# Linear attention into a gated attention layer: three products on quarters of the array's columns, feature weights first, other order

## Chip, cores and metric

The kernel runs on one core of a Trainium2 chip. The metric is the time of one execution in microseconds, measured on the device; lower is better. The engines of the core work side by side: TensorE (matmuls, PE in the rows; PEld are its weight loads), VectorE (DVE), ScalarE (ACT), GpSimd (POOL) and SyncE (SP), which issues the transfers here.

## What is computed

Eight batches of eight heads with 576 positions go through a linear attention, and its result through a layer of four masked attention experts, of which a gate takes two for each position. All is in f32.

```python
def phi(x):                                   # 64 -> 2 * 128 features
    proj = np.einsum('bhsd,df->bhsf', x, w_phi)
    proj = proj - np.max(np.abs(proj), axis=-1, keepdims=True)
    return np.concatenate([np.exp(proj), np.exp(-proj)], axis=-1)
q_p, k_p = (phi(q), phi(k))
kv = np.einsum('bhsf,bhsd->bhfd', k_p, v)
z = np.sum(k_p, axis=2)
num = np.einsum('bhsf,bhfd->bhsd', q_p, kv)
den = np.einsum('bhsf,bhf->bhs', q_p, z)[..., None] + 1e-06
x = num / den                                 # then (8, 576, 512)
...
logits = x @ w_gate                           # weights w of the best 2 of 4
for e in range(E):
    q, k, v = x @ wq[e], x @ wk[e], x @ wv[e]
    scores = np.where(causal, -1e9, scale * (q @ k.transpose(0, 2, 1)))
    a = softmax(scores)
    ye = a @ v @ wo[e]
    ...                                       # out += w * ye where e was taken
```

## The kernel before

The heads are taken in 32 pairs (`NPAIRS`, four to a batch); a pair has one head in partitions 0 to 63 and one in 64 to 127. For each pair `stream_k` projects the keys with the feature weights `wf` (L435 on two halves of the array's rows, the last 64 positions at L251), centres them on DVE and takes both exponentials on ACT into `ek`. `stream_kv` then multiplies the features with the values (L506), adds the sums over the keys (L523, the `z` of the reference, partly summed beforehand on DVE into `zs`), copies the result to `kvt`, transposes it (L532) and copies it to `kv`. `stream_q` projects the queries (L435), GpSimd finds the largest value over the features (L569), and DVE and ACT make the features `mx` and `u`. `stream_n` multiplies these with `kv`: first the denominators (L598), which go through a small transfer, a reciprocal and a broadcast on GpSimd, then the numerators (L607), which `divide` turns into `xh` and `xl`.

After four pairs a batch is complete. `stream_b` projects it for the experts (L251), makes the scores (L739, L251) and the exponentials `a`; `stream_t` scales and transposes these (L889), and `attend` multiplies them with the values `vs` (L920), 16 times in all. `project_out` (L251) ends the batch.

A matmul whose output has 64 partitions uses half of the array's columns, one with 32 a quarter; products that lie on different parts of the columns run side by side. Before, L506, L607 and L920 are on halves, L523 and L598 on quarters, L435 and L739 on two halves of the rows, and all else on the full array. I call each of these a tiling, and the step from one to another a change of tiling. One f32 product appears as two records of a weight load and a matmul. The sizes over positions are `PARTS`, 256 and 320.

The order of the work on each engine is fixed while the program is built. A `Plan` holds its own estimate of every engine's clock; each stream offers its next step with a position (`rank(p)` plus an entry of `POS1` or `NPOS`, or `at_batch(b)` plus one of `POS`, in units of a pair), and `loop` takes the ready step with the lowest position. A step on another tiling than the last one is put back by `OTHER`. While the first pairs fill the pipeline, `keep_warm` puts small matmuls without use into the gaps of TensorE; the last of them stands before the first finished pair. SP issues all loads in one queue, `load_phi` (the feature weights `wf`) among them, at position -5.

Of the kernel before, what the change touches and what calls it, by code (L numbers as in the profile page):

```python
# [39 lines left out]
ZEROS = 1.27   # L40

POS1 = {'k': -0.42, 'q': 0.49, 'v': 0.57, 'kv': 0.99, 'z': -1.95, 'cen': 0.77, 'evu': 0.02, 'ph0': -0.35, 'ph1': 0.01, 'div': 2.37, 'evd': -0.81, 'lk': -1.73, 'lq': -1.32} 
BOFF = (0.86, -0.14, 1.03, 0.96, 0.98, 0.78, -0.42, -2.05)

ORDER = (('p0', 'v0', 's0', 'p1', 's1'), ('p0', 'v0', 's0', 'p1', 's1'))
POS = {'p0': 7.38, 'p1': -0.11, 'v0': 7.93, 'gate': 6.05, 's0': 3.18, 's1': 6.21, 't0': 5.46, 't1': 9.4, 'out': 14.46} 
# [180 lines left out]
def tile_linear_attn_moe(ctx, tc, qt, kt, v, wts, out):  # L227
# [265 lines left out]
    def stream_kv():  # L493


        for p in range(NPAIRS):
# [3 lines left out]
            kc, ps = yield Step('PE', ekk + [vk], 'c', lambda: ('phi_k', p) in done and ('load_v', p) in done, tiling=(128, 64)), rank(p) + POS1['kv']  # L500
# [77 lines left out]
    def stream_n():  # L578


        for p in range(NPAIRS):
# [19 lines left out]
            for s0, s1 in PARTS:  # L601
                pk, ps = yield Step('PE', Pk + [kvk], 'c', has('rb', p), tiling=(128, 64)), rank(p) + NPOS[1]
                n = s1 - s0
                for c in range(2):
                    for h in range(2):
                        plan.run('PE', 2 * n / TRATE + 3, [pk], Pk + [kvk], tiling=(128, 64))
# [298 lines left out]
    def attend(b, g, pos):  # L905
# [7 lines left out]
        for s0, s1 in PARTS:  # L913
            pk, ps = yield Step('PE', AT, 'c', ready, tiling=(128, 64)), pos + SLOPE[3]
            js = range(0, (s1 + 127) // 128)
            for j in js:
                q0 = max(s0, 128 * j)
                for e in range(2):
                    plan.run('PE', 2 * (s1 - q0) / TRATE + 3, [pk], [f'vs{j}'] + AT, tiling=(128, 64))
# [113 lines left out]
```

## Time and profile before

| | |
|---|---|
| three runs | 659.52, 659.72, 660.65 us; median 659.72 |
| the profiled execution's own time | 662.2 us |
| span in that execution, first to last instruction | 660.4 us |
| TensorE, DVE, ACT, GpSimd busy | 98%, 81%, 72%, 31% of the span |
| mean granted TensorE clock | 1.000 |

The profile shows one execution. Times within it are counted from the span's start. A row of the timeline merges neighbouring records of one line, gives their count after the x, and the start of the first; the starts of two blocks that follow each other on TensorE give the duration of the first one with its change of tiling.

### The profile page before, as it was taken

To read this page: it belongs to the slowest core of one execution; us is meant where nothing else is said; L and a number is where in the kernel's file an instruction comes from. 1 tells how busy PE (TensorE), PEld (TensorE's weight loads), DVE (VectorE), ACT (ScalarE), POOL (GpSimd) and SP (SyncE) were. 2 spreads that over 40 slices of the span, in tenths; PEclk is the share of its full clock that TensorE was granted. 3 is DMA by queue.
4 is the path that set the end of the run, shared out by engine and by line. 5 is a ranking of instruction groups with operands and counts; after the bars stand their busy time and mean duration, and the time that the engine had idled before them with its cause. 6 is when DMAs were issued, how large, how long until landed. Compare 5 with 4: busy or idle time off the path is not lost.

```text
span 660.4 us, 16266 instructions
## 1 busy us (share of the span) xinstructions
PE 644.9 (98%) x6050; PEld 507.9 (77%) x6050; DVE 538.1 (81%) x1459; ACT 474.7 (72%) x1212; POOL 207.6 (31%) x154
## 2 busy tenths in 40 slices
PE   8999999999999999999999999999999999999997
PEld 7665677677887787777778787877888788888886
DVE  6889998889999778979899886997878986865562
ACT  4765868969777758668769885685877787765574
POOL 4717743172116162115332432122330523010000
PEclk9999999999999999999999999999999999999999
DMA  5643321021104022122221321113211210010011
GB/s 168 179 142 112 98 61 40 23 77 51 51 21 150 22 79 59 59 77 77 61 60 58 103 70 53 50 33 120 61 40 42 57 55 4 2 51 25 1 73 73
DMA packets 38752, 43.53 MB, mean 66 GB/s; under 512 B 19088, under 2 KB 21648, under 8 KB 38672
## 3 DMA queue, kind: packets, MB, share of 16 engines
q1 hardware_dynamic: 38672, 42.49, 21.8%
q8 instruction: 48, 0.79, 0.5%
q14 instruction: 32, 0.26, 0.1%
HBM read 32.58 MB, written 9.44 MB: 64 GB/s over the span
## 4 chain that ended last, share of the span: by engine, by line
PE 62%; DVE 19%; ACT 11%; issue 3%; DMA 2%; POOL 1%; SPq 1%; DVEq 0%; ACTq 0%
PE ps_c L251 21%; PE ps_c L607 7%; PE ps_c L506 7%; PE ps_c L435 7%; PE ps_c L889 6%; PE ps_c L920 5%; PE ps_c L598 4%; ACT a L262 3%; PE ps_c L739 3%; DVE ps_c L760 2%; DVE zs L465 2%; ACT ek L262 2%; DVE u L571 2%; DVE pmax L479 2%; PE ps_c L523 2%
## 5 line engine op out<-in xcount | busy, mean ns | idle before, releaser
L569 POOL PARTITION_ALL_REDUCE mx<-u x64 | 140.7, 2257 | 186.9 <-ACT u L260 180.7
L251 PE MATMUL ps_c<-xh,qk 128*128 128x320 f32 (+1 forms) x512 | 104.0, 294 | 0.0
L262 ACT ACTIVATE a<-ps_c,nm 128x256 f32<-128x256 f32 (+4 forms) x160 | 81.6, 526 | 27.0 <-DVE nm L760 15.0
L251 PEld LDWEIGHTS ps_c<-xh,qk 128*128 128x128 f32 x512 | 82.4, 188 | 0.4 <-DVE pmax L479 0.4
L262 ACT ACTIVATE ek<-ek 128x1152 f32<-128x1152 f32 x64 | 75.2, 1174 | 5.9 <-DVE ek L482 5.5
L639 POOL PARTITION_BROADCAST xf<-dr x32 | 30.7, 958 | 150.4 <-DMA dr<-dc 115.7
L506 PE MATMUL ps_c<-ek,v_in 128*64 128x256 f32 x640 | 75.1, 381 | 0.1
L251 PE MATMUL ps_c<-xl,qk 128*128 128x256 f32 (+1 forms) x256 | 75.1, 293 | 0.0
L760 DVE CUSTOM_DVE_ANT_0 ps_c<-ps_c,mask 128x128 f32<-128x128 f32 (+2 forms) x144 | 66.5, 517 | 2.1 <-PE ps_c L739 1.8
L479 DVE TENSOR_REDUCE pmax<-ps_c 128x4 f32<-128x512 f32 (+1 forms) x96 | 50.3, 547 | 20.0 <-PE ps_c L435 19.8
L506 PEld LDWEIGHTS ps_c<-ek,v_in 128*64 128x64 f32 x640 | 45.0, 137 | 27.0 <-ACT ek L262 1.1
L571 DVE TENSOR_TENSOR u<-u,mx 128x576 f32<-128x576 f32 x64 | 61.5, 970 | 4.1 <-POOL mx L569 4.0
L251 PE MATMUL ps_c<-vg,xh 128*128 128x260 f32 (+1 forms) x320 | 59.2, 286 | 0.0
L260 ACT COPY u<-ps_c 128x320 f32<-128x320 f32 (+1 forms) x122 | 40.9, 422 | 23.4 <-PE ps_c L435 23.1
L251 PE MATMUL ps_c<-yh,wo 128*128 128x256 f32 (+1 forms) x256 | 52.1, 298 | 1.4 <-ACT a L262 1.4
L889 PE MATMUL ps_c<-ident,a 128*128 128x128 f32 x400 | 49.7, 276 | 2.9 <-ACT a L262 2.2
L262 ACT ACTIVATE mx<-u 128x576 f32<-128x576 f32 x64 | 44.6, 696 | 10.2 <-DVE u L571 10.2
L889 PEld LDWEIGHTS ps_c<-ident,a 128*128 128x128 f32 x400 | 43.9, 141 | 9.6 <-ACT a L262 5.3
L482 DVE TENSOR_TENSOR ek<-ps_c,pmax 128x512 f32<-128x512 f32 (+1 forms) x96 | 50.9, 548 | 0.4
L260 ACT COPY at<-ps_c 128x128 f32<-128x128 f32 (+3 forms) x150 | 48.5, 460 | 0.7 <-PE ps_c L889 0.4
L251 PEld LDWEIGHTS ps_c<-xl,qk 128*128 128x128 f32 x256 | 48.1, 188 | 0.0
L251 PEld LDWEIGHTS ps_c<-vg,xh 128*128 128x128 f32 (+1 forms) x320 | 47.7, 178 | 0.1
(137 smaller groups left out, 1534.8 us busy)
## 6 DMA issues: line engine op xcount, KB each, us to landing
v_in<-in_v_dram SPq DMA_DIRECT2D x32, 320.0 KB, 3.0
q_in<-in_qt_dram SPq DMA_DIRECT2D x64, 144.0 KB, 2.9
out_dram<-ot SPq DMA_DIRECT2D x32, 288.0 KB, 2.2
k_in<-in_kt_dram SPq DMA_DIRECT2D x32, 160.0 KB, 2.9
k_in<-in_kt_dram SPq DMA_DIRECT2D x32, 128.0 KB, 2.8
dc<-dr SPq DMA_DIRECT2D x128, 2.2 KB, 1.9
ot<-in_wts_dram SPq DMA_DIRECT2D x5, 288.0 KB, 2.9
k_in<-in_kt_dram SPq DMA_DIRECT2D x32, 32.0 KB, 2.3
```

Of the source, the lines that this page charges most:

```text
L251: nc.tensor.matmul(o, a, b, start=start, stop=stop, skip_group_check=True)
L260: nc.scalar.copy(o, i)
L262: nc.scalar.activation(o, i, func, **kw)
L435: nc.tensor.matmul(o, a, b, start=True, stop=True, skip_group_check=True)
L479: dve(n * 128, [mk], [pk]).tensor_reduce(out=m[:, us], in_=src, axis=AX.X, op=ALU.max, apply_absolute_value=True)
L482: dve(n * 128, [f'ek{p % EKB}1'], [pk, mk]).tensor_tensor(out=ek2[p % EKB][:, 1, us, :], in0=src, in1=m[:, us].unsqueeze(2).to_broadcast([ ...
L506: nc.tensor.matmul(o[64 * h:64 * h + 64], v_in[:, 4 * h + t if t < 4 else 8 + h, :], ek[:, :, u_, :], start=t == 0, stop=t == 4, skip_grou ...
L569: nc.gpsimd.partition_all_reduce(M, U, 128, bass_isa.ReduceOp.absmax)
L571: dve(S, [uk], [mk], port=True).tensor_tensor(out=U, in0=U, in1=M, op=ALU.subtract)
L607: nc.tensor.matmul(ps[64 * h:64 * h + 64, 0:n], kvi[:, c, 64 * h:64 * h + 64], P_[h][c][:, s0:s1], start=c == 0, stop=c == 1, skip_group_c ...
L760: dve(n, [('nm', g, c), pk], [pk]).tensor_tensor_reduce(out=src, in0=src, in1=m, scale=-1.0, scalar=3.0e38, op0=ALU.add, op1=ALU.min, accu ...
L889: nc.tensor.transpose(ps[:, n * 128:(n + 1) * 128], a_blk[c][:, j, :], ident)
```

## The change

The three products on halves are each divided into two on quarters, over the same operands, and the plan's costs follow. The feature weights' load moves to position -50, ahead of all others. The numbers that set the order (`HOT`, `SLOPE`, `NPOS`, `FLEX`, `POS1`, `BOFF`, `POS`, `HEAD`, `OTHER`) are others; of these the diff keeps a few lines.

```diff
-HOT = 4.41 
-SLOPE = (0.61, 1.58, 5.89, 0.14, 0.85) 
+HOT = 4.2 
+SLOPE = (1.17, 1.58, 5.87, 0.13, 0.98) 
...
-HEAD = 4.01
+HEAD = 2.83
-OTHER = 2.37
+OTHER = 3.21
...
             for t in range(NJ):
                 for h in range(2):
                     u_ = 4 * h + t if t < 4 else 8
-                    plan.run('PE', 2 * 256 / TRATE + 3, [kc], ekk + [vk], tiling=(128, 64))
-                    nc.tensor.matmul(o[64 * h:64 * h + 64], v_in[:, 4 * h + t if t < 4 else 8 + h, :], ek[:, :, u_, :],
-                                     start=t == 0, stop=t == 4, skip_group_check=True)
+                    for k in range(2):
+                        g = slice(64 * h + 32 * k, 64 * h + 32 * k + 32)
+                        plan.run('PE', 256 / TRATE + 2, [kc], ekk + [vk], tiling=(128, 32))
+                        nc.tensor.matmul(o[g], v_in[:, 4 * h + t if t < 4 else 8 + h, 32 * k:32 * k + 32], ek[:, :, u_, :],
+                                         start=t == 0, stop=t == 4, skip_group_check=True)
...
                 for c in range(2):
                     for h in range(2):
-                        nc.tensor.matmul(ps[64 * h:64 * h + 64, 0:n], kvi[:, c, 64 * h:64 * h + 64],
-                                         P_[h][c][:, s0:s1], start=c == 0, stop=c == 1, skip_group_check=True)
+                        for g in range(64 * h, 64 * h + 64, 32):
+                            nc.tensor.matmul(ps[g:g + 32, 0:n], kvi[:, c, g:g + 32], P_[h][c][:, s0:s1], start=c == 0, stop=c == 1,
+                                             skip_group_check=True)
...
                 for e in range(2):
-                    nc.tensor.matmul(ps[64 * e:64 * e + 64, q0 - s0:s1 - s0], vs[j][:, g, e, :], ats[j][:, e, q0 - 128 * j:s1 - 128 * j],
-                                     start=j == 0, stop=j == js[-1], skip_group_check=True)
+                    for k in range(2):
+                        nc.tensor.matmul(ps[64 * e + 32 * k:64 * e + 32 * k + 32, q0 - s0:s1 - s0], vs[j][:, g, e, 32 * k:32 * k + 32],
+                                         ats[j][:, e, q0 - 128 * j:s1 - 128 * j], start=j == 0, stop=j == js[-1], skip_group_check=True)
...
-    for gen, pos in ((load_phi(), -5), ...
+    for gen, pos in ((load_phi(), -50), ...
```

In the changed kernel the lines shift: L506, L523, L532, L598, L607, L739, L889 and L920 become L508, L525, L534, L600, L610, L742, L892 and L924.

The first place is SP's queue at the start of the program, before; a row is one issue of a transfer, to the left of the arrow where it goes (`k_in`, `q_in` and `v_in` are keys, queries and values of a pair).

```order
L283 DMA k_in_105<-in_kt_dram 64x640
L283 DMA k_in_105<-in_kt_dram 64x512
L283 DMA k_in_105<-in_kt_dram 64x128
L283 DMA q_in_107<-in_qt_dram 64x576 x2
L283 DMA wf<-in_wts_dram 128x128
L283 DMA k_in_106<-in_kt_dram 64x640
L283 DMA k_in_106<-in_kt_dram 64x512
L283 DMA k_in_106<-in_kt_dram 64x128
L283 DMA q_in_108<-in_qt_dram 64x576 x2
L283 DMA v_in_109<-in_v_dram 128x640
```

The feature weights stand sixth, behind the first pair's keys and queries. The same queue in the changed kernel:

```order
L283 DMA wf<-in_wts_dram 128x128
L283 DMA k_in_105<-in_kt_dram 64x640
L283 DMA k_in_105<-in_kt_dram 64x512
L283 DMA k_in_105<-in_kt_dram 64x128
L283 DMA q_in_107<-in_qt_dram 64x576 x2
L283 DMA k_in_106<-in_kt_dram 64x640
L283 DMA k_in_106<-in_kt_dram 64x512
L283 DMA k_in_106<-in_kt_dram 64x128
L283 DMA v_in_109<-in_v_dram 128x640
L283 DMA q_in_108<-in_qt_dram 64x576 x2
```

They now stand first, and the second pair's queries come behind the first pair's values.

The second place is TensorE's queue around the 21st pair's product of features and values, before (`ps_c` are the banks of PSUM; the size is output partitions by columns, and x4 counts matmuls in a row).

```order
L739 MATMUL ps_c_66<-kkh_176,ql_173 128x384
L506 MATMUL ps_c_65<-ek_111,v_in_109 64x256 x10
L523 MATMUL ps_c_65<-zs,ones 32x128 x4
L607 MATMUL ps_c_67<-mx_138,kv_122 64x256
...
L607 MATMUL ps_c_68<-u_131,kv_122 64x320
L598 MATMUL ps_c_62<-mx_140,kv_123 32x256
...
L598 MATMUL ps_c_64<-u_133,kv_123 32x320
L739 MATMUL ps_c_61<-kkh_176,qh_172 128x512
```

The tilings follow as row halves, column halves, quarters, column halves, quarters, row halves; the transposes of this `kvt` (L532) come 90 rows behind L523. The same pair in the changed kernel:

```order
L742 MATMUL ps_c_63<-kkh_176,ql_173 128x512
L610 MATMUL ps_c_61<-mx_138,kv_122 32x256 x2
...
L610 MATMUL ps_c_66<-u_131,kv_122 32x320 x2
L600 MATMUL ps_c_68<-mx_140,kv_123 32x256
...
L600 MATMUL ps_c_62<-u_133,kv_123 32x320
L508 MATMUL ps_c_65<-ek_111,v_in_109 32x256 x20
L525 MATMUL ps_c_65<-zs,ones 32x128 x4
L435 MATMUL ps_c_61<-wf,k_in_106 128x128
...
L251 MATMUL ps_c_66<-wf,k_in_106 128x128
L534 MATMUL ps_c_65<-ident,kvt 128x128 x3
```

Numerators, denominators, features by values and key sums now follow each other on quarters, and the transposes of `kvt` come 13 projections behind the key sums.

## Rows read from the trace of the kernel before

**Rows 1.** The page's busy time of each engine (us, share of the span, instructions), and its chain of work that ended last, as shares of the span by engine and by line.

```profile
PE 644.9 (98%) x6050; PEld 507.9 (77%) x6050; DVE 538.1 (81%) x1459; ACT 474.7 (72%) x1212; POOL 207.6 (31%) x154
...
PE 62%; DVE 19%; ACT 11%; issue 3%; DMA 2%; POOL 1%; SPq 1%; DVEq 0%; ACTq 0%
PE ps_c L251 21%; PE ps_c L607 7%; PE ps_c L506 7%; PE ps_c L435 7%; PE ps_c L889 6%; PE ps_c L920 5%; PE ps_c L598 4%; ACT a L262 3%; PE ps_c L739 3%; DVE ps_c L760 2%; DVE zs L465 2%; ACT ek L262 2%; DVE u L571 2%; DVE pmax L479 2%; PE ps_c L523 2%
```

**Rows 2.** Windows: the stretch in us and its length, then busy time (and instructions) of PE, PEld, DVE, ACT and POOL, the granted clock, the share of the DMA engines, GB/s.

```profile
60.00:120.00 60.00, 58.57 (x525) 42.73 (x525) 56.08 (x136) 46.77 (x107) 31.47 (x22) 1.00 0.22 60
...
240.00:360.00 120.00, 118.80 (x1101) 94.41 (x1099) 106.29 (x284) 89.35 (x225) 43.06 (x31) 1.00 0.23 68
360.00:480.00 120.00, 119.72 (x1135) 93.80 (x1133) 101.08 (x269) 89.76 (x228) 36.38 (x26) 1.00 0.23 67
```

**Rows 3.** Groups of instructions by line, operation and shape: their count, busy time in us and mean ns of one, and the idle time before them.

```profile
L506 PE MATMUL ps_c<-ek,v_in 128*64 128x256 f32 x640 | 75.1, 381 | 0.1
...
L262 ACT ACTIVATE ek<-ek 128x1152 f32<-128x1152 f32 x64 | 75.2, 1174 | 5.9 <-DVE ek L482 5.5
```

**Rows 4.** TensorE's timeline from 284.9 to 293.2 us: start, duration to the last end, line, operands, rows*columns of the array, operand size, count of records. L607 stands between two blocks on halves.

```profile
284.92 2.93 PE L920 MATMUL ps_c<-at,vs 128*64 128x256 f32 x28
287.67 0.60 PE L607 MATMUL ps_c<-mx,kv 128*64 128x256 f32 x4
...
289.62 2.33 PE L506 MATMUL ps_c<-ek,v_in 128*64 128x256 f32 x20
291.87 0.42 PE L523 MATMUL ps_c<-zs,ones 128*32 128x128 f32 x8
292.12 0.38 PE L598 MATMUL ps_c<-mx,kv 128*32 128x256 f32 x1
...
292.33 0.38 PE L598 MATMUL ps_c<-mx,kv 128*32 128x256 f32 x1
...
292.55 0.43 PE L598 MATMUL ps_c<-mx,kv 128*32 128x320 f32 x1
...
293.20 1.16 PE L435 MATMUL ps_c<-wf,k_in 64*128 64x128 f32 x16
```

**Rows 5.** The same view from 246.9 us: L607 comes from the full array and goes on to L506.

```profile
246.90 0.65 PE L607 MATMUL ps_c<-mx,kv 128*64 128x256 f32 x4
...
248.89 0.82 PE L506 MATMUL ps_c<-ek,v_in 128*64 128x256 f32 x6
```

**Rows 6.** The same view from 337.2 us: L506, L523, L607 and L598, each with another tiling than the one ahead of it.

```profile
337.23 2.38 PE L506 MATMUL ps_c<-ek,v_in 128*64 128x256 f32 x20
339.54 0.43 PE L523 MATMUL ps_c<-zs,ones 128*32 128x128 f32 x8
339.89 0.65 PE L607 MATMUL ps_c<-mx,kv 128*64 128x256 f32 x4
...
341.98 0.40 PE L598 MATMUL ps_c<-mx,kv 128*32 128x256 f32 x1
...
342.22 0.38 PE L598 MATMUL ps_c<-mx,kv 128*32 128x256 f32 x1
...
342.44 0.43 PE L598 MATMUL ps_c<-mx,kv 128*32 128x320 f32 x1
...
343.09 0.50 PE L739 MATMUL ps_c<-kkh,qh 64*128 64x512 f32 x2
```

**Rows 7.** The timeline of all engines from the start of the span; SPq rows are issues of transfers, in brackets the idle time before and what ended it.

```profile
0.72 1.86 SPq L283 DMA_DIRECT2D k_in<-in_kt_dram  x3
...
2.62 1.24 SPq L283 DMA_DIRECT2D q_in<-in_qt_dram  x2
...
3.90 0.59 SPq L283 DMA_DIRECT2D wf<-in_wts_dram  x1
...
6.40 2.08 PE L435 MATMUL ps_c<-wf,k_in 64*128 64x128 f32 x16 [1.02 <-DMA wf<-in_wts_dram]
...
8.24 2.04 PE L435 MATMUL ps_c<-q_in,wf 64*128 64x256 f32 x8
...
10.83 15.89 POOL L569 PARTITION_ALL_REDUCE mx<-u  x7 [8.83 <-ACT u L260]
```

**Rows 8.** The page's DMA issues: transfer, count, KB each, median us from issue to landing.

```profile
q_in<-in_qt_dram SPq DMA_DIRECT2D x64, 144.0 KB, 2.9
...
k_in<-in_kt_dram SPq DMA_DIRECT2D x32, 160.0 KB, 2.9
k_in<-in_kt_dram SPq DMA_DIRECT2D x32, 128.0 KB, 2.8
```

**Rows 9.** TensorE's waits: who waited for whom, us in total, times, the longest in us.

```profile
PE ps_c L251 <- ACT a L262: 3.1, 4, 1.4
PE ps_c L532 <- ACT kvt L260: 2.4, 3, 1.1
PE ps_c L889 <- ACT a L262: 2.2, 6, 0.7
```

**Rows 10.** ACT's timeline: one copy of the products of features and values out of PSUM.

```profile
328.26 0.48 ACT L260 COPY kvt<-ps_c 128x384 f32<-128x384 f32 x1
```

**Rows 11.** The chain that ended last, in order of time (start, us, what): the projections of a pair's keys and queries.

```profile
293.27 2.06 PE ps_c L435 x24
```

More of the change, by code (lines that the diff above doesn't have):

```diff
@@ L28 @@
 PXB = 6
-HOT = 4.41
-SLOPE = (0.61, 1.58, 5.89, 0.14, 0.85)
-NPOS = (-0.32, 2.07)
+HOT = 4.2
+SLOPE = (1.17, 1.58, 5.87, 0.13, 0.98)
+NPOS = (1.07, 2.1)
 UB = 4
 AB = 1
-FLEX = (154, -44)
+FLEX = (151, -50)
 QB = 1
@@ L40 @@
 ZEROS = 1.27
-POS1 = {'k': -0.42, 'q': 0.49, 'v': 0.57, 'kv': 0.99, 'z': -1.95, 'cen': 0.77, 'evu': 0.02, 'ph0': -0.35, 'ph1': 0.01, 'div': 2.37, 'evd': -0.81, 'lk': -1.73, 'lq': -1.32}
-BOFF = (0.86, -0.14, 1.03, 0.96, 0.98, 0.78, -0.42, -2.05)
+POS1 = {'k': -0.42, 'q': 0.3, 'v': 0.35, 'kv': 0.68, 'z': -1.84, 'cen': 1.1, 'evu': 0.51, 'ph0': -0.21, 'ph1': 0.01, 'div': 2.66, 'evd': -0.83, 'lk': -1.07, 'lq': -0.41}
+BOFF = (0.78, 1.0, 1.0, 1.02, 0.8, 0.67, -0.27, -2.25)
 ORDER = (('p0', 'v0', 's0', 'p1', 's1'), ('p0', 'v0', 's0', 'p1', 's1'))
-POS = {'p0': 7.38, 'p1': -0.11, 'v0': 7.93, 'gate': 6.05, 's0': 3.18, 's1': 6.21, 't0': 5.46, 't1': 9.4, 'out': 14.46}
+POS = {'p0': 7.06, 'p1': 1.33, 'v0': 9.25, 'gate': 5.43, 's0': 3.27, 's1': 6.09, 't0': 3.9, 't1': 9.4, 'out': 14.92}
 NPAIRS = B * NP
-HEAD = 4.01
+HEAD = 2.83
 ADDS = (0, 2)
@@ L499, in stream_kv @@
             ek, ekk = ek2[i], [f'ek{i}0', f'ek{i}1']
-            kc, ps = yield Step('PE', ekk + [vk], 'c', lambda: ('phi_k', p) in done and ('load_v', p) in done, tiling=(128, 64)), rank(p) + POS1['kv']
+            kc, ps = yield Step('PE', ekk + [vk], 'c', lambda: ('phi_k', p) in done and ('load_v', p) in done, tiling=(128, 32)), rank(p) + POS1['kv']
             o = ps[:, 0:256].rearrange("p (c f) -> p c f", c=2)
@@ L601, in stream_n @@
             for s0, s1 in PARTS:
-                pk, ps = yield Step('PE', Pk + [kvk], 'c', has('rb', p), tiling=(128, 64)), rank(p) + NPOS[1]
+                pk, ps = yield Step('PE', Pk + [kvk], 'c', has('rb', p), tiling=(128, 32)), rank(p) + NPOS[1]
                 n = s1 - s0
@@ L605, in stream_n @@
                     for h in range(2):
-                        plan.run('PE', 2 * n / TRATE + 3, [pk], Pk + [kvk], tiling=(128, 64))
-                        nc.tensor.matmul(ps[64 * h:64 * h + 64, 0:n], kvi[:, c, 64 * h:64 * h + 64],
-                                         P_[h][c][:, s0:s1], start=c == 0, stop=c == 1, skip_group_check=True)
+                        for g in range(64 * h, 64 * h + 64, 32):
+                            plan.run('PE', n / TRATE + 2, [pk], Pk + [kvk], tiling=(128, 32))
+                            nc.tensor.matmul(ps[g:g + 32, 0:n], kvi[:, c, g:g + 32], P_[h][c][:, s0:s1], start=c == 0, stop=c == 1,
+                                             skip_group_check=True)
                 plan.spawn(divide(p, s0, s1, pk, ps), rank(p) + POS1['div'])
@@ L913, in attend @@
         for s0, s1 in PARTS:
-            pk, ps = yield Step('PE', AT, 'c', ready, tiling=(128, 64)), pos + SLOPE[3]
+            pk, ps = yield Step('PE', AT, 'c', ready, tiling=(128, 32)), pos + SLOPE[3]
             js = range(0, (s1 + 127) // 128)
@@ L918, in attend @@
                 for e in range(2):
-                    plan.run('PE', 2 * (s1 - q0) / TRATE + 3, [pk], [f'vs{j}'] + AT, tiling=(128, 64))
-                    nc.tensor.matmul(ps[64 * e:64 * e + 64, q0 - s0:s1 - s0], vs[j][:, g, e, :], ats[j][:, e, q0 - 128 * j:s1 - 128 * j],
-                                     start=j == 0, stop=j == js[-1], skip_group_check=True)
+                    for k in range(2):
+                        plan.run('PE', (s1 - q0) / TRATE + 2, [pk], [f'vs{j}'] + AT, tiling=(128, 32))
+                        nc.tensor.matmul(ps[64 * e + 32 * k:64 * e + 32 * k + 32, q0 - s0:s1 - s0], vs[j][:, g, e, 32 * k:32 * k + 32],
+                                         ats[j][:, e, q0 - 128 * j:s1 - 128 * j], start=j == 0, stop=j == js[-1], skip_group_check=True)
             plan.spawn(evac_y(b, g, s0, s1, pk, ps), pos)
@@ L967, in evac_o @@
             done.add(('out', 4 * b + t))
-    for gen, pos in ((load_phi(), -5), (keep_warm(), 1e9), (zeros(), ZEROS), (load_k(), -1), (load_q(), -1), (load_v(), -1), (stream_k(), 0), (stream_q(), 0),
+    for gen, pos in ((load_phi(), -50), (keep_warm(), 1e9), (zeros(), ZEROS), (load_k(), -1), (load_q(), -1), (load_v(), -1), (stream_k(), 0), (stream_q(), 0),
                      (weights(w_qk, ('w', 1)), 1.5), (weights(w_vg, ('w', 2)), 2.5),
```

## Prediction

> **What bounds the kernel now.** I read the page's busy times and its chain first, then the windows, then TensorE's groups by form, its timeline at three places, its waits, and the first microseconds. TensorE is busy for 644.9 of 660.4 us, DVE for 81% [rows 1]. The windows say that this is no average over unlike stages: from 60 us on TensorE is busy 58.57 of 60 and 118.80 and 119.72 of 120, at a granted clock of 1.00 [rows 2]. So TensorE's own work sets the time, and what it does between the matmuls counts too. But the chain that ended last runs over TensorE for only 62% of the span; of the three lines that change it holds 7%, 7% and 5% (L607, L506, L920) [rows 1]. Elsewhere DVE or ACT released TensorE with hardly any slack: a microsecond taken from TensorE there comes back as a wait.
>
> **The products themselves: 0.** One f32 product is two records on TensorE: the 320 products of `stream_kv` show as 640 records [rows 3]. Two halves run side by side. A block of 20 half records with 256 columns, entered from blocks that are also on halves, lasts from 289.62 to 291.87, of which the last 0.09 or 0.10 belongs to the change that follows: 2.16 us, 0.216 for a pair of records [rows 4]. Four quarters run side by side too: at L598 sets of four records with 256 columns start at 292.12, 292.33 and, with the next ones, 292.55 [rows 4], again 0.216 a set. Four quarter records do the work of two half records, so the doubled count of instructions should cost nothing as long as a set lasts 0.216. The weight loads hide behind the running set; what it costs where they do not is a rival below. Shorter records are bounded by issue: eight L523 records took 291.87 to 292.12, 31 ns each [rows 4], so a set of four needs at most 0.125 us. Only the sets of 64 columns in `attend` (0.054 at the rate above) could fall short of it, by 0.07 twice in each of 16 calls, 2 us at the worst. I take 0 because L523's 31 ns is set by its 128 columns as much as by issue; 2 goes into the range.
>
> **The changes of tiling: TensorE's work falls by 6.3 us.** A block of 16 records at L607 lasts 1.95 us where it comes from halves (L920) and goes on to halves (L506) [rows 4]; 1.99 where it comes from full tiles and goes on to halves [rows 5]; 2.09 where it comes from quarters and goes on to quarters [rows 6]. Entering halves thus costs 0.05 and leaving a tiling 0.10, in sum 0.15 a change. Entering quarters costs 0.025 in place of 0.05: the first set at L598 takes 0.24 to the next when it comes from L607 (341.98, 342.22), the second 0.22 [rows 6]. By the two orders, with the warming matmuls left out, 202 changes of tiling become 160. Into halves there were 51, now none. Into quarters there were 44, now 47. Into row halves and the full array there were 107, now 113. So 51 x 0.15 = 7.65 goes, and 3 x 0.125 = 0.4 and 6 x 0.15 = 0.9 come: 7.65 - 1.3 = 6.3 us. At 0.10 a change, the drain alone, it would be 4.2. The place in the order shown above has it all: five changes before (row to half, to quarter, to half, to quarter, to row), two after.
>
> **What of it reaches the end: 4.4.** L607 has 32 blocks of about 2.0 us, 64 us, and 7% of 660.4 = 46 us on the chain [rows 1]: 0.72. L506 has 32 x 2.25 = 72 us and again 46: 0.64. L920 has 16 x 2.75 = 44 us [rows 4] and 5% = 33: 0.75. I take 0.7 x 6.3 = 4.4 us. Ends: 0.62 (TensorE's whole share) of 4.2 us of work, 2.6, and all 6.3.
>
> **Feature weights first: 1.0.** `wf` was issued sixth, at 3.90, and TensorE waited for it until 6.40 [rows 7]. Issued first, it pushes the key and query loads back by one issue, 0.59. The two key pieces that the first products read are then issued at 1.3 and 1.9 and land some 2.8 or 2.9 later [rows 8], at 4.8: 1.6 us earlier than 6.40. The queries land at 3.8 + 2.9 = 6.7 [rows 8], when the key products (8.24 - 6.40 = 1.84 us) are over. GpSimd's first reduction, at 10.83 [rows 7], moves up by about 1.5, and early on GpSimd holds the pace. Past 30 us TensorE is full; of the 1.5 I take 1.0, between 0 and 1.6. The second pair's queries now queue behind one more load, `v_in`, 0.59; GpSimd has two reductions of 15.89 / 7 = 2.27 us to do in that time [rows 7], so I put it at nothing (0.6 if not covered).
>
> **The other order: 0, between -4 and +4.** Idle time on TensorE is 660.4 - 644.9 = 15.5 us; its named waits are mostly for ACT: 3.1 (L251), 2.4 (L532), 2.2 (L889) [rows 9]. The new order puts more of its own work ahead of some of these and less ahead of others (the kvt rival). Without a row for it, half of these 7.7 could go, or be added once more.
>
> **Sum.** 4.4 + 1.0 + 0 = 5.4 us. The profiled execution took 662.2 (span 660.4 and 1.8 around it): 656.8 for the changed kernel. The median of the runs lies 2.5 below the profiled one, so the forecast is 659.72 - 5.4 = **654.3 us**, 0.8% faster. 0.2% (1.3 us) is about what a measurement of this kernel can tell from no change.
>
> **Rivals.** *Saving swallowed (0.12):* DVE is busy 56.08 of 60 us between 60 and 120 us [rows 2], and where the chain goes over DVE and ACT the saved TensorE time turns into waits. Then TensorE's busy share falls to 97%, its idle time grows by about 5, and the time is 658.5 to 661. Against: the changed lines lie on the chain for two thirds of their time.
>
> *Transposes of kv too soon (slower, 0.11):* behind the key denominators (L523) the copy `kvt` leaves PSUM on ACT, 0.48 us [rows 10], and then TensorE transposes it (L532). By the two orders, with row durations, in 18 of the last 26 pairs 3.0 us of TensorE's work or less stands between, often 24 records of L435 (2.06 [rows 11]) and one product of `wf`; before, in 2 of them. If ACT is in one of its 1174 ns exponentials [rows 3], or in a pair of them, the copy starts late and TensorE stands. The point from which it decides: ACT busy for over some 2.7 - 0.48 - 0.5 = 1.7 us after the last denominator. Three such waits made 2.4 us before, the longest 1.1 [rows 9]. At 18 x 0.6 = 11 us the kernel would take 654.3 + 11 = 665. For it: the distance. Against: in ACT's new order only one of 30 such copies stands right behind an exponential of the keys.
>
> *Weight loads not hidden (slower, 0.03):* twice as many loads, of 32 columns. If each set took 0.24 as the first one behind a change does [rows 6] and not 0.216: 10 sets x 32 + 8 x 32 + 14 x 16 = 800 sets x 0.024 = 19 us, so 673. That the products gain nothing and lose is decided by the second set behind a change; L598's took 0.22 [rows 6], hence the small chance. *Issue-bound (slower, 0.01):* were L523's 31 ns a record the pace of light records only, and twice that the pace with other operands, a set of four quarters would need 0.25 us. Then the sets of 256 columns lose 0.032, 320 times in `stream_kv` and 128 times in `stream_n` (14 us), and the short sets of `attend` together 0.9 in each of 16 calls (14 us): 654.3 + 28 = 682. L523's eight records took 0.25 us with eight weight loads between them [rows 4], so I give it 0.01. The Trainium skill, TensorE: Matmul & The Clock Gate (section "Wait — 56ns, not 53.3ns?"), has a rule of this kind: with hardware decode off the sequencer spends about 62 ns on each matmul; as an estimate by that page a set would take 0.248, and the kernel would be slower by nearly what this rival gives. By that rule eight records of L523 would take 0.5 us, and the trace has 0.25: it does not hold there.
>
> **How the numbers follow.** Forecast 0.73, with 649 to 658.4 of its own: TensorE's whole 6.3 with 1.6 of the head and half of the waits gone gives 659.7 - 11 = 648.7; 2.6 with nothing else gives 657.1. Swallowed 0.12, kvt 0.11, loads 0.03, issue 0.01. The range reaches from 649.0 to 660.8, past the swallowed case, and leaves out the slow ones and the outermost gain. Faster by over 0.2%: 0.74 (the forecast, and a sliver of the swallowed case); within: 0.12; slower: 0.14.
>
> **What would show it.** Right: blocks of the three products last as long as before, less 0.15 for each change; the L508 block behind L600 starts its sets 0.216 apart from the first on; no start gap of 0.1 between L508 and L525; the first L435 near 4.8 us; TensorE's idle time within 4 us of 15.5. Wrong: sets at 0.24 or more (loads), waits at L534 for ACT's kvt of over 5 us (kvt rival), or a DVE share above 82% with TensorE at 97% (swallowed). The prediction fails as a whole if new waits on TensorE add up to more than 4 us.

## The result and the profile after

| | before | after |
|---|---|---|
| median of 5 runs | 660.65 us (659.52 to 661.20) | 664.85 us (662.88 to 665.04) |
| profiled execution, its span | 662.20, 660.4 | 664.99, 663.2 |
| idle time of TensorE in that span | 15.5 | 19.3 |
| mean granted clock of TensorE | 1.000 | 0.994 |

The ratio is 1.0059 with an interval of [1.0048, 1.0071]: slower by 0.6%, outside the range and on the other side of the forecast. Of all the runs in this document one, of 2204 us, was disturbed and is not counted.

The page after, its busy times and its chain (for [rows 1]):

```profile
PE 643.9 (97%) x7653; PEld 503.6 (76%) x7653; DVE 532.4 (80%) x1464; ACT 474.2 (72%) x1207; POOL 204.4 (31%) x154
...
PE 58%; DVE 18%; ACT 10%; DMA 4%; issue 3%; SPq 3%; POOL 2%; DVEq 0%; ACTq 0%; POOLq 0%
```

TensorE's busy time fell by 1.0 and not by 6, its idle time grew by 3.8, and the chain now runs over transfers and their issues for 7%, where it was 3%. What the change does to the products is not the reason. TensorE's timeline in the changed kernel at one block of `stream_kv` (for [rows 4]):

```profile
292.96 2.34 PE L508 MATMUL ps_c<-ek,v_in 128*32 128x256 f32 x40
295.12 0.40 PE L525 MATMUL ps_c<-zs,ones 128*32 128x128 f32 x8
```

Forty quarter records start and the next line follows 2.16 us later, as twenty halves took without the change behind them; the group of L508 is busy for 75.1 us, as L506 was in [rows 3]. The time went elsewhere. TensorE's waits (for [rows 9]):

```profile
PE ps_c L892 <- ACT a L262: 3.3, 7, 0.8
PE ps_c L525 <- DVE zs L470: 2.9, 4, 1.0
PE ps_c L435 <- DMA q_in<-in_qt_dram: 2.0, 2, 1.8
PE ps_c L534 <- ACT kvt L260: 1.7, 2, 0.9
...
PE ps_c L251 <- ACT a L262: 1.0, 1, 1.0
```

The wait for the queries is new, and that for the sums `zs` has grown (0.3 us before). Others went: that of L251 for `a` was 3.1 us [rows 9], and that for `wf` 1.0 [rows 7]. The queries are those of the second pair, in the timeline of the head (for [rows 7]):

```profile
4.24 2.23 PE L435 MATMUL ps_c<-wf,k_in 64*128 64x128 f32 x15
...
6.24 0.58 SPq L283 DMA_DIRECT2D v_in<-in_v_dram  x1
...
6.87 1.10 SPq L283 DMA_DIRECT2D q_in<-in_qt_dram  x2
...
8.21 4.26 POOL L571 PARTITION_ALL_REDUCE mx<-u  x2 [6.22 <-ACT u L260]
...
12.70 1.46 PE L435 MATMUL ps_c<-q_in,wf 64*128 64x256 f32 x6 [1.78 <-DMA q_in<-in_qt_dram]
...
14.20 4.26 POOL L571 PARTITION_ALL_REDUCE mx<-u  x2 [1.72 <-ACT u L260]
```

and the times from issue to landing of the queries' first eight loads:

```profile
DMA to landing us min/median/max: 2.8/3.2/5.2
```

The first key product starts at 4.24 in place of 6.40 and GpSimd's first reduction at 8.21 in place of 10.83, better than forecast. But the second pair's queries, two loads, are issued from 6.87 on behind `v_in`. The second of the two takes the 5.2 us, and TensorE goes on only at 12.70. It stands for 1.78 us, GpSimd, which ran seven reductions without a pause before, for 1.72 after two of them, and the lead is spent. The second place is at 64 to 76 us, in the timeline of all engines:

```profile
63.67 2.37 PE L508 MATMUL ps_c<-ek,v_in 128*32 128x256 f32 x40
64.75 1.21 DVE L465 TENSOR_TENSOR zs<-ek 128x1024 f32<-128x1024 f32 x1
65.38 1.30 POOL L642 PARTITION_BROADCAST xf<-dr  x1 [3.98 <-DMA dr<-dc]
...
65.99 1.09 DVE L467 TENSOR_TENSOR zs<-zs 128x512 f32<-128x512 f32 x1
66.77 1.04 POOL L644 PARTITION_BROADCAST xf<-dr  x1
67.12 2.26 DVE L470 TENSOR_TENSOR zs<-zs,ek 64x256 f32<-64x256 f32 x2
67.77 4.29 POOL L571 PARTITION_ALL_REDUCE mx<-u  x2
68.00 0.41 PE L525 MATMUL ps_c<-zs,ones 128*32 128x128 f32 x4 [0.79 <-DVE zs L470]
69.44 0.41 PE L525 MATMUL ps_c<-zs,ones 128*32 128x128 f32 x4 [1.02 <-DVE zs L470]
70.71 0.55 PE L534 MATMUL ps_c<-ident,kvt 128*128 128x128 f32 x3 [0.86 <-ACT kvt L260]
...
73.61 1.08 PE L610 MATMUL ps_c<-mx,kv 128*32 128x256 f32 x8
74.47 0.86 PE L610 MATMUL ps_c<-u,kv 128*32 128x256 f32 x8
```

VectorE's additions run beside GpSimd's broadcasts and reduction and are late, TensorE stands three times, and then a block of L610 that elsewhere has its next block 0.43 us behind it has it 0.86 behind. The windows say why (columns as in [rows 2]; the granted clock is the number behind the busy times):

```profile
13.50:16.90 3.40, 3.40 (x27) 2.62 (x26) 0.00 (x0) 3.28 (x7) 2.70 (x2) 0.50 0.59 163
68.00:71.60 3.60, 1.72 (x17) 1.01 (x19) 3.57 (x7) 1.27 (x5) 3.60 (x2) 0.99 0.42 106
71.60:75.00 3.40, 3.40 (x32) 2.26 (x32) 3.40 (x7) 2.20 (x2) 1.25 (x2) 0.50 0.22 74
```

After each of the two places the granted clock is 0.50, the lower of its two levels (1.2 of 2.4 GHz), for 3.4 us. The two stretches hold 3.4 us of TensorE's work less than at 1.00, most of the 5.3 that its busy time did not fall by. Some 1.5 us of the first stretch are warming matmuls without use, so less than that reaches the products.

### The profile page after: what moved, and what is told of

Same layout as the page of the kernel before. It is cut to its first block, busy times and chain, and to the rows that moved or that the text cites. A ratio compares the mean times of both kernels' runs of the same rounds, so it can differ in the third digit from the quotient of the medians.

```text
span 663.2 us, 19465 instructions
## 1 busy us (share of the span) xinstructions
PE 643.9 (97%) x7653; PEld 503.6 (76%) x7653; DVE 532.4 (80%) x1464; ACT 474.2 (72%) x1207; POOL 204.4 (31%) x154
## 4 chain that ended last, share of the span: by engine, by line
PE 58%; DVE 18%; ACT 10%; DMA 4%; issue 3%; SPq 3%; POOL 2%; DVEq 0%; ACTq 0%; POOLq 0%
PE ps_c L251 20%; PE ps_c L610 7%; PE ps_c L508 7%; PE ps_c L435 6%; PE ps_c L892 6%; PE ps_c L924 5%; PE ps_c L742 4%; PE ps_c L600 3%; SPq L283 3%; DVE u L573 3%; ACT ek L262 2%; ACT a L262 2%; DMA dc<-dr 2%; DVE zs L465 2%; DVE ps_c L763 2%
## 5 line engine op out<-in xcount | busy, mean ns | idle before, releaser
L571 POOL PARTITION_ALL_REDUCE mx<-u x64 | 139.3, 2224 | 155.8 <-ACT u L260 147.1
L251 PE MATMUL ps_c<-xh,qk 128*128 128x320 f32 (+1 forms) x512 | 104.5, 294 | 0.0
L251 PEld LDWEIGHTS ps_c<-xh,qk 128*128 128x128 f32 x512 | 82.5, 188 | 0.5 <-DVE u L573 0.4
L508 PE MATMUL ps_c<-ek,v_in 128*32 128x256 f32 x1280 | 75.1, 380 | 0.1
L251 PE MATMUL ps_c<-xl,qk 128*128 128x256 f32 (+1 forms) x256 | 75.0, 293 | 0.0
L508 PEld LDWEIGHTS ps_c<-ek,v_in 128*32 128x32 f32 x1280 | 40.7, 110 | 30.4 <-issue 0.6
L573 DVE TENSOR_TENSOR u<-u,mx 128x576 f32<-128x576 f32 x64 | 57.1, 900 | 5.0 <-POOL mx L571 4.9
L251 PE MATMUL ps_c<-vg,xh 128*128 128x260 f32 (+1 forms) x320 | 59.9, 287 | 0.5 <-ACT u L260 0.2
L260 ACT COPY u<-ps_c 128x256 f32<-128x256 f32 (+1 forms) x123 | 41.1, 419 | 24.3 <-PE ps_c L435 23.9
L892 PE MATMUL ps_c<-ident,a 128*128 128x128 f32 x400 | 50.1, 276 | 3.7 <-ACT a L262 3.3
L251 PE MATMUL ps_c<-yh,wo 128*128 128x256 f32 (+1 forms) x256 | 51.5, 296 | 0.0
L892 PEld LDWEIGHTS ps_c<-ident,a 128*128 128x128 f32 x400 | 43.9, 141 | 8.8 <-ACT a L262 6.2
L251 PEld LDWEIGHTS ps_c<-vg,xh 128*128 128x128 f32 (+1 forms) x320 | 47.4, 178 | 1.8 <-ACT u L260 1.1
L251 PEld LDWEIGHTS ps_c<-xl,qk 128*128 128x128 f32 x256 | 48.1, 188 | 0.0
L260 ACT COPY at<-ps_c 128x128 f32<-128x128 f32 (+2 forms) x139 | 45.7, 460 | 1.4 <-PE ps_c L892 1.2
```

Of the source, the lines that this page charges most:

```text
L251: nc.tensor.matmul(o, a, b, start=start, stop=stop, skip_group_check=True)
L260: nc.scalar.copy(o, i)
L508: nc.tensor.matmul(o[g], v_in[:, 4 * h + t if t < 4 else 8 + h, 32 * k:32 * k + 32], ek[:, :, u_, :], start=t == 0, stop=t == 4, skip_grou ...
L571: nc.gpsimd.partition_all_reduce(M, U, 128, bass_isa.ReduceOp.absmax)
L573: dve(S, [uk], [mk], port=True).tensor_tensor(out=U, in0=U, in1=M, op=ALU.subtract)
L892: nc.tensor.transpose(ps[:, n * 128:(n + 1) * 128], a_blk[c][:, j, :], ident)
```

## The experiments

Sixteen kernels. To hold one thing while another is changed, the sequence of steps that the planner chose (stream, engine, banks of PSUM) was written out as a list for each kernel and followed word for word; "the old order" is that of before, "the new order" that of after, and an edit of the order moves entries of the list. Line numbers there are some 82 higher (L607 is L525 of after, L616 is L534, L552 is L470). Each ratio is to the kernel before, run in turn with it on the same chip; its medians were 661.01, 661.39, 660.64 and 661.06 us in the four sessions. Kernels of different sessions are best compared by their ratios; 0.001 is 0.66 us.

### 1. The parts of the change

**Quarters alone, in the old order.** The plan of before, the products of after.

> The quarters alone: the products on quarters, every engine's order step for step that of the kernel before (feature weights sixth, as there). 47 changes of tiling between halves and quarters are gone, 39 x 0.12 + 8 x 0.15 = 5.9 us, and 43 entries to quarters in place of halves save 0.025 each, in sum 7.0 us of TensorE's work. Theory order (the quarters save as predicted, and the other order loses it): 4.4 to 7.0 us faster than the kernel before, 653.5 to 656. Theory swallowed (whatever TensorE saves comes back as waits for DVE and ACT): within 1.3 us of the kernel before.

658.63 us (657.22 to 660.03), ratio 0.9962 [0.9950, 0.9974]. Between the two forecasts: 2.4 us reach the end, a third of the 7.0 us of TensorE's work that were counted for this order, and about half of the 4.4 that the prediction took.

**The new order alone, with halves.**

> The other order alone: every engine's order step for step that of the changed kernel, the products on halves as before. The new order brings quarters and halves together that the old one kept apart: 243 changes of tiling against 160. Theory order: 83 changes at 0.12 to 0.15 plus 51 dearer entries come on top of the changed kernel, about 11 us, 673 to 677, since the order loses about 10 us by itself. Theory swallowed: most of those 11 us vanish in the waits that are there already, 665 to 669.

671.80 us (669.08 to 672.20), 1.0153 [1.0132, 1.0173], again between the two forecasts. The new order, with the feature weights' earlier load in it, costs 11 us with halves and, by 664.85 - 658.63, 6 with quarters: the order of after suits its quarters, but is worse than the old one for both.

**The second pair's queries first.** The new order with two entries changed:

```diff
-load_v 0
 load_q 1
+load_v 0
```

> The changed kernel with one step of SP's queue put back: the second pair's queries are issued ahead of the first pair's values, all else as it is. In the changed kernel TensorE waits until 12.7 us for them. Theory head (320 KB of values ahead of them cost 1.6 us, TensorE stands, its granted clock falls to half at 13.4 us, and about 1 us of it lasts): the wait falls to under 0.5 us, the clock stays full up to 30 us, and the kernel is 0.5 to 1.5 us faster than the changed one. Theory middle (all of the loss arises later, at 65 to 75 us): within 0.5 us of the changed kernel, with the clock still falling at 71 us.

661.95 us (658.42 to 664.13), 1.0006 [0.9989, 1.0022]: 2.9 us less than after, twice the head theory's upper end. Beside the changed kernel on one chip (below) it was 1.8. In the trace the wait for the queries is gone and the clock is full up to 30 us; it fell later, at 153.7 us.

**The feature weights alone, in the old order**, with quarters.

```diff
+load_phi 0
 load_k 0
 load_q 0
-load_phi 0
```

> The quarters in the old order with the feature weights issued first and nothing else moved: the sequence wf, keys, queries, keys, queries, values. Theory of the prediction (the head moves up by 1.5 us and 1.0 of it lasts): 0.7 to 1.6 us faster than quarters_old_order. Rival (the first pairs are paced by what all loads together bring in, and not by the first product): within 0.5 us of it.

658.26 us (657.90 to 658.45), 0.9956 [0.9943, 0.9969]: 0.4 less than without, as the rival had it, and not told apart from it. This is the profile in which the swallowing can be read, since it has the steps of before one for one. Some rows of TensorE's timeline, first before:

```profile
22.24 0.55 PE L532 MATMUL ps_c<-ident,kvt 128*128 128x128 f32 x3 [1.06 <-ACT kvt L260]
...
82.32 0.41 PE L523 MATMUL ps_c<-zs,ones 128*32 128x128 f32 x4 [0.26 <-DVE zs L470]
...
153.82 2.62 PE L889 MATMUL ps_c<-ident,a 128*128 128x128 f32 x22 [0.27 <-ACT a L262]
...
644.38 2.96 PE L889 MATMUL ps_c<-ident,a 128*128 128x128 f32 x23 [0.72 <-ACT a L262]
```

and the same steps here:

```profile
21.09 0.55 PE L616 MATMUL ps_c<-ident,kvt 128*128 128x128 f32 x3 [1.10 <-ACT kvt L342]
...
80.23 0.41 PE L607 MATMUL ps_c<-zs,ones 128*32 128x128 f32 x4 [0.23 <-DVE zs L552]
...
152.27 2.62 PE L974 MATMUL ps_c<-ident,a 128*128 128x128 f32 x22 [0.27 <-ACT a L344]
...
640.31 2.96 PE L974 MATMUL ps_c<-ident,a 128*128 128x128 f32 x23 [0.72 <-ACT a L344]
```

The lead is 1.15 us at 22 us (the weights), 2.09 at 82, 1.55 at 154 and 4.07 at 644. It is that of two single executions; by the medians the whole gain is 2.75. The windows from the first of these steps to the third, and from there to the last, are, before:

```profile
22.24:153.82 131.58, 129.13 (x1301) 91.01 (x1301) 117.72 (x273) 101.21 (x228) 61.01 (x39) 1.00 0.29 84
153.82:644.38 490.56, 484.29 (x4453) 391.21 (x4453) 401.53 (x1132) 357.06 (x950) 133.72 (x100) 1.00 0.19 55
```

and here, with the page's busy times:

```profile
21.09:152.27 131.18, 126.70 (x1673) 89.61 (x1674) 119.50 (x274) 100.94 (x228) 57.78 (x39) 1.00 0.31 86
152.27:640.31 488.04, 481.11 (x5633) 385.82 (x5634) 400.20 (x1132) 356.73 (x950) 133.76 (x100) 1.00 0.19 56
...
PE 638.6 (97%) x7650; PEld 500.3 (76%) x7650; DVE 539.3 (82%) x1459; ACT 474.2 (72%) x1212; POOL 205.9 (31%) x154
```

TensorE's busy time falls by 6.3 in the whole (644.9 before). Up to 154 us it falls by 2.4, and the stretch gets shorter by 0.4; from there on it falls by 3.2, and the stretch gets shorter by 2.5. The waits in these rows are as long as before. What grew up to 100 us are others, those for `kvt` above all: 3.5 us in five places, where before had 2.4 in three [rows 9].

### 2. Single waits taken away

**The transposes of kv later**, in the old order (weights first) and in the new one (queries first); `stream_kv`'s transposes of pairs 4 and 5 go behind the next pair's key products, in the old order those of pair 7 too, behind two steps of scores:

```diff
-stream_kv, transposes of pair p
 stream_k, key products of the next pair
+stream_kv, transposes of pair p
```

> Quarters in the order of before with the feature weights first (658.26 us), with three steps of TensorE moved: the key-value transposes of pairs 4 and 5 stand behind the next pair's key products (1.65 us of work), those of pair 7 behind the next two score steps. In the run without the move TensorE waited there 0.67, 0.88 and 0.70 us for ScalarE's copy. If the saving of the quarters was swallowed by waits that only the order of TensorE's steps makes, the three waits go and most of 2.2 us reaches the end: 656.0 to 657.0. If VectorE and ScalarE bound the stage (another wait takes their place at once, of zs or of ek), the time stays within 0.5 us of 658.3.

> The changed kernel with the second pair's queries loaded ahead of the first pair's values (661.95 us), with the key-value transposes of pairs 4 and 5 moved behind the next pair's key products on TensorE. There the transposes followed the sums' products at once and TensorE waited 0.86 us for ScalarE's copy both times. If the order's cost is that nothing stands between the two, 1.7 us come back, more if the granted clock then falls less often: 658.8 to 660.5. If the stage is bound elsewhere (VectorE's sums zs), the waits move on and the time stays at 661 to 662.5.

658.01 us (656.90 to 658.77), 0.9949 [0.9934, 0.9964], and 662.19 (660.86 to 663.26), 1.0010 [1.0000, 1.0021]. Both stayed where they were. The waits for `kvt` went, and others took their place. In the old order:

```profile
PE ps_c L590 <- ACT ek L344: 1.2, 1, 1.2
PE ps_c L607 <- DVE zs L552: 1.1, 3, 0.5
...
PE ps_c L616 <- ACT kvt L342: 0.6, 2, 0.4
```

against 0.2, 0.6 and 3.5 us without the move. So these three places in TensorE's order do not bound the stage of the pairs.

**The waits filled**, new order with the queries first. Products whose results are overwritten stand where TensorE waits: ahead of the `kvt` transposes of pairs 4 and 5 (shown), ahead of the first two groups of transposes of `a`, and among the key sums of pair 5.

```diff
+for _ in range(8): nc.tensor.transpose(ps[:, 0:128], ident, ident)
 nc.tensor.transpose(ps[:, 128 * c:128 * c + 128], kvt[:, c, :], ident)
```

> The same kernel (661.95 us) with TensorE's longest waits filled by products whose results are overwritten: eight transposes of the identity (0.9 us) ahead of the key-value transposes of pairs 4 and 5, and ahead of the first two groups of transposes of the first group's attention, where the granted clock fell at 153.7 us, and fourteen sets of four quarter products (1.5 us) in the sums of pair 5. Nothing that waits comes earlier by it. If the fall of the granted clock to half is what makes part of the loss, it stays at 1.0 here and the time is 659.0 to 660.7, as the runs of that kernel at a clock of 1.000 (658.4, 660.6). If the clock has nothing to do with these waits, or the fillers cost what the clock gives, it stays at 661.3 to 663.5 with means of 0.994 to 0.997.

662.17 us (661.23 to 664.03), 1.0021 [1.0009, 1.0033]. The mean clock was 0.999 or 1.000 in 9 of 12 runs, against 3 of 12 without the fillers, and 3 of 12 with the transposes moved, on the same chip as this: with TensorE kept busy it falls less often. But the median did not follow. Among these runs the nine at the full clock took 661.23 to 663.70 us and the three at 0.996 or 0.997 663.71 to 664.03, so the fillers may have cost what the clock gave. That was not measured by itself: undecided for the price.

**GpSimd's broadcasts left out**, the two of pair 2, in the new order with the queries first; the products of that pair are multiplied by other numbers.

> The same kernel (661.95 us) without GpSimd's two broadcasts of pair 2 (1.6 and 0.9 us; the products of that pair are then multiplied by other numbers). In its trace they ran at 60.16 to 62.68 us, beside VectorE's additions into zs, which took 1.09 and 2.02 us there, against 0.69 and 0.87 where GpSimd was idle, and TensorE waited 0.59 and 1.19 us for zs. If GpSimd's work beside VectorE is what made zs late, the additions of pair 5 fall to 0.7 and 0.9 us (the second perhaps slowed by the all-reduce that follows), the two waits to under 0.5 us together, and the time by 1 to 2 us: 660 to 661. If VectorE's additions are late by their place in the order alone, they keep their lengths or TensorE its waits, and the time stays at 661.5 to 662.5.

661.06 us (659.49 to 663.68), 0.9997 [0.9983, 1.0011]: 0.9 less, 0.6 by the ratios, under the 1 to 2 forecast and, as the intervals overlap, not told apart from no gain. In the trace the mechanism is plain:

```profile
61.70 1.21 DVE L547 TENSOR_TENSOR zs<-ek 128x1024 f32<-128x1024 f32 x1
62.95 0.69 DVE L549 TENSOR_TENSOR zs<-zs 128x512 f32<-128x512 f32 x1
63.67 0.87 DVE L552 TENSOR_TENSOR zs<-zs,ek 64x256 f32<-64x256 f32 x2
64.14 0.87 PE L607 MATMUL ps_c<-zs,ones 128*32 128x128 f32 x8
64.72 4.27 POOL L653 PARTITION_ALL_REDUCE mx<-u  x2 [6.31 <-ACT u L342]
```

The 1.09 and 2.02 us of the kernel with the queries first have become 0.69 and 0.87, and L607 follows its blocks without a wait at this place. Part of it came back as a wait for `ek` (1.4 us).

### 3. Is it VectorE that bounds the pairs' stage?

From 20 to 100 us VectorE is busy for 72.7 of the 80 us before, 71.5 after and 74.3 with quarters in the old order (weights first): 89 to 93%.

**The output weights prepared later**, at 140 to 180 us in place of 45 to 68.

> Quarters in the order of before with the feature weights first (658.26 us), and the preparation of the output weights (two loads of TensorE-ready copies: four operations on VectorE and ScalarE, some 2.6 us, at 45 to 57 us) moved as a whole to 140 to 180 us; they are needed at 205 us. VectorE was busy 74.3 of the 80 us from 20 to 100 us. If VectorE bounds that stage, most of the 1.4 to 2 us that it is relieved of comes back: 656.4 to 657.3. If the stage is bound by TensorE's order and its single waits, the time stays within 0.5 us of 658.3.

> The changed kernel with the second pair's queries ahead of the first pair's values (661.95 us), with the same move of the output weights' preparation (at 48 to 68 us there) to about 140 to 180 us. VectorE was busy 74.7 of the 80 us from 20 to 100 us. If VectorE bounds that stage: 660.0 to 661.0 (more if the clock then falls less often). If not, 661.5 to 662.5.

658.59 us (657.79 to 659.20), 0.9969 [0.9957, 0.9982]: no gain in the old order, a miss for VectorE as the only bound. 660.02 us (659.19 to 662.16), 0.9996 [0.9985, 1.0007] in the new one (queries first), just inside VectorE's forecast by the median, but by the ratios only 0.7 less than without the move, with intervals that overlap; TensorE waits 1.1 us for `zs` in place of 3.2.

**VectorE's sums of pairs 5 to 7 left out**, in the old order; the products of the sums then use those of pair 4.

```diff
+if p not in (5, 6, 7):
     dve(1024, ['zs'], ekk, port=True).tensor_tensor(...)
     ...
```

> Quarters in the order of before (658.63 us) without VectorE's sums of the keys of pairs 5 to 7 (three operations and 2.8 to 4.5 us each pair; the sums' products then use those of pair 4). With its twin in halves it asks whether VectorE is what swallowed the quarters' saving up to 100 us. If VectorE bounds the stage, this kernel gains more from the relief than the halves do and the two end 3.5 to 5.0 us apart, against 2.4 with the sums. If the saving is lost elsewhere, they stay 2.0 to 3.0 apart, whatever the relief gives both.

> The kernel before (661.0 us), in its own order, without VectorE's sums of the keys of pairs 5 to 7. If VectorE bounds the stage already in halves: 658 to 660. If TensorE does, and VectorE only for the quarters: 660.3 to 661.3, while the twin in quarters falls to 656 to 657.5.

Quarters 657.15 us (655.73 to 658.89), 0.9951 [0.9935, 0.9967]; halves 660.80 (659.10 to 662.51), 0.9996 [0.9984, 1.0009]. The two are 3.7 us apart by the medians, which speaks for VectorE as what swallowed the quarters' saving, but 3.0 by the ratios, and with their intervals that decides nothing. Halves gain nothing that shows from the relief, as forecast for TensorE as the bound there. The traces say more, by the windows between the same steps as above, up to the third of them (halves, then quarters):

```profile
20.35:150.79 130.44, 128.09 (x1303) 90.49 (x1302) 109.52 (x262) 100.84 (x227) 59.06 (x39) 1.00 0.31 87
21.84:151.56 129.72, 126.05 (x1673) 89.75 (x1674) 107.73 (x261) 100.52 (x228) 58.86 (x40) 1.00 0.31 87
```

VectorE is busy for 83% there, and of 2.0 us that TensorE's busy time falls by, 0.7 come through. With the sums it was 0.4 of 2.4 (weights first); with quarters alone the stretch even got longer by 0.4, though TensorE's busy time fell by 2.5. So VectorE's sums are at most a part of what swallows the saving.

**The new order on one chip**, four kernels together.

> The changed kernel as it is, on the chip of the next three, as what they are compared with: 664 to 665.5, a ratio of about 1.006 to the kernel before.

> The changed kernel with the preparation of the output weights moved from 45 to 68 us to about 140 to 180 us, and nothing else. If VectorE is what makes the sums late, 1.0 to 2.5 us less than the changed kernel beside it (its waits for zs of 2.9 us fall to about 1.1, and the granted clock no longer falls at 71.6 us). If the gain seen with the second queries first was the chip's, within 0.7 us of it.

> The changed kernel with the second pair's queries ahead of the first pair's values, on this chip: 2.0 to 3.5 us less than the changed kernel beside it if the first runs held; under 1.5 us if the difference was the chip's.

> The same with the queries first, without VectorE's sums of the keys of pairs 5 to 7 (the sums' products then use those of pair 4). If VectorE bounds the stage of the pairs in the new order: 2 to 4 us less than the kernel with the queries first beside it, and no wait for zs before 100 us. If TensorE's own order does: within 1 us of it, with other waits in their place.

| new order, quarters | us (lowest to highest) | ratio to before |
|---|---|---|
| as changed | 664.01 (663.26 to 665.78) | 1.0051 [1.0035, 1.0067] |
| output weights later | 663.44 (662.00 to 665.19) | 1.0040 [1.0022, 1.0058] |
| queries first | 662.18 (661.02 to 665.12) | 1.0026 [1.0013, 1.0039] |
| queries first, no sums of pairs 5 to 7 | 660.41 (658.86 to 663.05) | 0.9993 [0.9981, 1.0006] |

The output weights alone gave 0.6, within the rival's 0.7, although in that trace the waits for `zs` fell from 2.9 to 1.3 us and the clock stayed at 0.999. That was the fastest of its seven runs, 662.00; the three at 0.999 or 1.000 took 662.00 to 663.19, the others, at 0.995 to 0.997, 663.44 to 665.19. The queries gave 1.8, between the two forecasts. Leaving out the sums gave 1.8 more, a little under the 2 to 4 forecast, with intervals that do not meet; no wait for `zs` was left before 100 us, while the two waits for `kvt` stayed (2.0 us). VectorE's late sums are thus a part of the new order's cost in this stage, and not all of it. Leaving them out also took work away, which in the old order was worth 0.7 us by the ratios (0.9962 to 0.9951).

**What the clock costs.** The twelve runs of the kernel with the queries first on this chip, sorted by their mean granted clock: at 0.996 and 0.997 seven took 661.02 to 662.20 us, at 0.994 three took 662.81 to 663.83, at 0.992 two 664.24 and 665.12. That is 1.6 us for each 0.0025, about one stretch of 3.4 us at 0.50, which is 1.7 us of TensorE's work. The runs were only sorted, so the waits ahead of a fall are in these differences too. Where it falls differs from run to run; in the first profile of that kernel it fell here (TensorE's timeline, then the windows):

```profile
152.42 0.33 PE L974 MATMUL ps_c<-ident,a 128*128 128x128 f32 x1 [0.84 <-ACT a L344]
153.35 4.29 PE L974 MATMUL ps_c<-ident,a 128*128 128x128 f32 x22 [0.61 <-ACT a L344]
```

```profile
153.70:157.10 3.40, 3.40 (x18) 3.40 (x17) 2.34 (x6) 3.06 (x7) 0.00 (x0) 0.50 0.21 36
157.10:162.00 4.90, 4.90 (x71) 3.38 (x73) 3.40 (x7) 4.29 (x14) 1.41 (x1) 1.00 0.24 70
```

## Why the prediction was wrong, step by step

- **The products, 0:** right. Sets of four quarters start 0.216 us apart, and the 64-column sets of `attend` 0.056 apart. The weight-load and issue rivals fell with it: the next line starts 0.33 us after eight L525 records do, change of tiling included. The 62 ns that the Trainium skill, TensorE: Matmul & The Clock Gate (section "Wait — 56ns, not 53.3ns?"), gives for a matmul with hardware decode off would make 0.5 of them, and are not seen here.
- **The changes of tiling, 6.3 us of TensorE's work:** the count was about right: in the old order, where 7.0 were counted, TensorE's busy time fell by 6.3, and the gap behind L508 is gone as forecast. With the new order held, halves to quarters takes 8.6 us off TensorE's busy time (652.5 to 643.9) and 7 off the time (671.80 to 664.85).
- **"0.7 of it reaches the end":** this step failed in the old order, where 2.4 us came through. The 0.7 was a mean over the span, from how much of each line lies on the chain. In the traces 0.4 of 2.4 us came through from 22 to 154 us and 2.5 of 3.2 from there on. In the first stretch a wait taken from TensorE returned as another. That VectorE, 93% busy from 20 to 100 us, does this is not shown: with less work for it the old order gained nothing once and 1.5 us at most the other time, and two thirds of the saving were swallowed with VectorE at 83%.
- **The other order, "0, between -4 and +4":** this step failed most. It cost 6 us with quarters (11 with halves). It was treated as unknowable from both sides, though the order of after could be read. Shown as its parts: the queries behind the first values (1.8 to 2.9) and VectorE's late sums `zs` (1.8, some of which any order would gain by leaving them out), with the falls of the clock that follow such waits contained in both. The rest, 2 us or more (660.41 against 658.26, where the old order still has its sums), is open. There are single waits of 0.6 to 1.0 us that the old order does not have, at 333 (`zs`), 497 and 553 us, but others have gone: between these two kernels' traces TensorE's idle time is 16.7 against 17.7 us, and its busy time 641.0 against 638.6, at a clock of 0.999 and 1.000. So the rest lies in what counts as TensorE's busy time. By the counts it has five changes of tiling more (160 against 202 - 47 = 155), at most 0.75 us of it.
- **Feature weights first, 1.0:** the first products came 2.2 us earlier, more than the 1.6 forecast, but of the gain nothing was kept after the change. The failing term is the second pair's queries, which "now queue behind one more load", put "at nothing (0.6 if not covered)". The load ahead of them was priced by its issue, 0.59. It has 320 KB, and the second of the two query loads landed 5.2 us after its issue, where 2.9 is the median [rows 8]; with the queries ahead of the values the wait was gone. In the old order with weights first the lead of 1.15 us at 22 us is there, and the medians show 0.4.
- **The rivals:** kv transposes too soon did not happen as such: waits at L534 for `kvt` are 1.7 us, not 11, and without them the time is the same. The swallowed case had the right mechanism for the quarters, and quarters in the old order took 658.63, at the edge of its 658.5 to 661; that was forecast for the whole change, which left that range on the slow side. None had the granted clock: it was 1.00 in all windows read before, so that a standstill could lower it was in no row.
- **The signs named ahead:** waits that are new add up to more than 4 us (`zs` 2.6 more, queries 2.0), the condition under which the prediction "fails as a whole". A sign of being right came true all the same, TensorE's idle time within 4 us of 15.5 (19.3), since other waits went. It does not see work at half the clock, which counts as busy.
- **The sums:** the lower end of the forecast adds 6.3, 1.6 and half of 7.7, which is 11.75 and not 11: 648.0 in place of 648.7. It changes nothing here.

The fastest kernels found that do the whole work are quarters in the old order with the weights first, 658.26 us, and with the transposes moved as well, 658.01; they beat both kernels, by 0.4 and 0.5% against before, and are not told apart from one another.

## What to carry to other kernels

When a change comes with a new order, cost the order before the arithmetic: list at each engine's head which transfer now stands ahead of which, priced by when it lands and not by its issue alone, and which additions on VectorE are needed at once and run beside GpSimd. A share of the chain is a mean; of a saving on the busiest engine most passes through in one stage (here 2.5 of 3.2 us after 154 us) and hardly any in another (0.4 of 2.4 before). And where TensorE stands for one to two microseconds, read the clock behind it too.

## What the runs showed of the hardware

- The granted clock of TensorE fell to 0.50 in stretches of 3.4 us behind waits of 0.84 and 0.61 us (at 152 us), of 0.79, 1.02 and 0.86 (at 67 to 71 us) and of 1.78 (at 12 us). Such waits are not always followed by a fall: 0.84 and 0.61 at 151 us were not in the profile without the sums. A mean clock of 0.997 or less is seen in most runs of the new order and few of the old. Each stretch holds 1.7 us less of TensorE's work.
- VectorE's additions into `zs` slowed down beside GpSimd: 512 columns 0.69 us alone and 1.09 beside a broadcast, the two of 256 columns together 0.87 alone and 2.26 beside a broadcast and a reduction. GpSimd's broadcast was longer too, 1.0 to 1.6 us against 0.86. The old order has such additions as well: all of them together take 91.4 us there (weights first) and 92.8 in the new order (queries first).
- Four products on quarters ran at the pace of two on halves, 0.216 us a set (75.1 us for either group), with twice the weight loads and no gap for them.
